# Attention, a 2-D FFT and a feed-forward: batch 1's first rows beside batch 0's spectral part, weights converted a whole piece at a time, tables loaded later

## The chip, the cores and the metric

One core of a Trainium2 chip. The time is device time in microseconds (us) of one launch. The engines of the core run side by side, each from its own queue in order: PE (TensorE: matmuls and transposes, into PSUM banks), DVE (VectorE), ACT (ScalarE), POOL (GpSimd), and SP, whose queue issues the DMAs. PEld is PE's loading of weights.

## The reference

```python
# q, k, v: (8, 12, 448, 64); w_ch1: (768, 3072); w_ch2: (3072, 768)
q_n, k_n = rmsnorm(q, g_q), rmsnorm(k, g_k)            # over the last axis
attn = softmax(q_n @ k_n.T / sqrt(64))                 # 448 x 448 per head
x = (attn @ v).transpose(0, 2, 1, 3).reshape(8, 448, 768)
mixed = real(fft(fft(x, axis=1), axis=2))
u = x + mixed
un = (u - mean(u)) / sqrt(var(u) + 1e-6)               # over the 768
out = u + maximum(un @ w_ch1, 0) @ w_ch2
```

All in float32; the weights arrive as 64-bit floats and are read as pairs of 32-bit words.

## The kernel before

The eight batches go through three parts each. `attention` works on pairs of heads (six pairs p): `transpose_pair` loads and normalises q and k (`norm_pair`: POOL raises the sums of squares to -1/2, tile ss; qkn is the product) and turns them into QT and KD; `softmax_pair` makes scores in four blocks of 112 rows (c), two heads each, tiles S: DVE takes the minimum of the negated scores (mn), ACT the exponential with its sum (P, sm), and P is scaled; `value_pair` transposes P (pt, copied to T) and multiplies by v (av) into xT. `fold` then adds and subtracts mirrored columns of xT (sd, eo, tot; DVE), and `spectral` does the two Fourier steps as matmuls with tables, D1 (tiles y, copied to Y) and D2 (tiles ab, joined to smdf), adds the residual (x, u) and normalises (un). `ffn` multiplies by the two weights: 24 pieces of w1 (tiles h, 18 matmuls each) and 36 of w2 (tiles o, 12 each). Where three matmuls stand for one, a float32 operand was split into a rounded part and a remainder.

A weight piece is converted once, during batch 0. `convert` loads the 64-bit words (dblw, line 650), then: ACT two operations (653, 654), DVE three (655, 659, 663, into magw), POOL an addition (667), ACT a rounding copy (668), POOL a subtraction (669), which gives the rounded part and the remainder (w). `converted` calls it for the two halves of a piece and stores the result in DRAM, from where later batches load it (line 713). The raw words lie in buffers "X", four of half a piece. 14 pieces (eight of w1, six of w2) are converted during batch 0's attention and spectral part (`convert_some`; their tiles have an e in the name), the other 46 during batch 0's feed-forward, up to three pieces of each weight ahead of use.

The order of work is that of Python generators: batch 0's `aux` (attention, then spectral) runs alone with the early conversions; then `merge` runs `ffn(b)` beside `aux(b + 1)`, a step of the one or the other by a ratio of costs. `aux(1)` begins there. A scheduler then places the instructions on each engine's queue by a timeline of its own, within the dependencies. PSUM banks are shared by tag: "S" (two banks) serves the scores, half of the y tiles, and all ab tiles.

`load_dft` is called at the second step of batch 0: it loads D1 and, as a staging tile d2s of 113 rows in one DMA, the second table; ACT rounds it into D2 and DVE forms the remainder.

Of the kernel before, what the change touches and what calls it, by code (L numbers as in the profile page):

```python
# [11 lines left out]
F32 = mybir.dt.float32  # L12
# [30 lines left out]
EARLY = 2  # L43
PLAIN_PAIRS = range(NPAIR)
# [43 lines left out]
def spectral_block(ctx, tc, q, k, v, g_q, g_k, w1, w2, d1, d2, out, nb=B):  # L88
# [63 lines left out]
    SLOTS = {"P": 8, "PT": 6, "X": 4, "M": 2, "unT": 6, "h": 6}  # L152

    def slot(tag, name, dtype=F32):
        return sb.tile([128, 900], dtype, tag=tag, name=name, bufs=SLOTS[tag])

# [12 lines left out]
    KL = cpool.tile([128, 2, S], F32R, name="KL")  # L169
# [8 lines left out]
    D2 = cpool.tile([N1, 2, 2, 2, N1], F32R, name="D2")  # L178
# [9 lines left out]
    def load_dft():  # L188
        nc.sync.dma_start(D1.rearrange("r i a n -> r (i a n)"), d1)
        st = slot("PT", "d2s")[:N1, : 4 * N1].rearrange("s (n t) -> s n t", n=4)  # L190
        nc.sync.dma_start(st, d2.rearrange("s (n t) -> s n t", n=4))
        d2v = D2.rearrange("s i c a t -> s (i c) a t")
        A.copy(d2v[:, :, 0], st)
        sub(d2v[:, :, 1], st, d2v[:, :, 0])
# [7 lines left out]
    FOLD_SLOTS = (("unT", "unT"), ("PT", "P"), ("M", "X"))  # L202
# [177 lines left out]
    def value_pair(b, p, Pc, xT):  # L380
# [6 lines left out]
        if plain(b, p):  # L387
# [3 lines left out]
            for h, a in enumerate((lo, hi)):  # L391
                av = bank("either" if b == 0 else "av", f"av{b}_{p}_{h}")
                for j in range(3):
                    pt = bank("PT", f"pt{b}_{p}_{h}_{j}")
                    for c in range(NC):
                        nc.tensor.transpose(
                            pt[:, c * C : (c + 1) * C],
                            Pc[c][:, 512 * h + j * 128 : 512 * h + (j + 1) * 128],
                            ident[:C, :C],
                        )  # L400
                    T = slot("PT", f"T{b}_{p}_{h}_{j}")[:, :S]
                    if (h * 3 + j) % 2 == 0:
                        V.tensor_copy(T, pt[:, :S])
                    else:
                        A.copy(T, pt[:, :S])
                    nc.tensor.matmul(
                        av[:D, :S], vhl[:, j, h], T, start=j == 0, stop=False
                    )
                    yield 1180
                nc.tensor.matmul(  # L410
                    av[:D, :S], vhl[a, 3, h], R[a], start=False, stop=True
                )
                A.copy(xT[a, p, :S], av[:D, :S])
                yield 760
# [35 lines left out]
    def attention(b, xT, EO):  # L450
# [3 lines left out]
        for p in range(NPAIR):  # L454
# [13 lines left out]
            if p > 3 and b != 1:  # L468
                fold(b, p - 4, xT, EO)
                yield 0  # L470
            values = value_pair(b, p, Pc, xT)
# [3 lines left out]
        for p in range(0 if b == 1 else 2, 3):  # L475
            fold(b, p, xT, EO)
# [3 lines left out]
    rstds = {}  # L480

    def fold(b, p, xT, EO):
# [5 lines left out]
        eo = slot(kept, f"eo{b}_{p}").rearrange("r (i t) -> r i t", i=2)  # L488
# [137 lines left out]
    uns = {}  # L626

    def aux(b):

        xT = sb.tile([128, NR, S + 2], F32, tag="xT", name=f"xT{b}", bufs=1)  # L630
        EO, uns[b] = [], {}
        yield from attention(b, xT, EO)
        yield from spectral(b, xT, EO, uns[b])
# [8 lines left out]
    def convert(src, bits, part, name):  # L642
# [4 lines left out]
        raw = slot("X", f"dbl{name}", U32)[:, : c * f].rearrange(  # L647
# [25 lines left out]
    class Stream:  # L673
# [18 lines left out]
        def converted(self, i, name):  # L692
# [5 lines left out]
            for c in (slice(0, self.n // 2), slice(self.n // 2, self.n)):  # L698
                convert(
                    src[:, c], bits[:, c], [hl[:, k, c] for k in range(2)],  # L700
                    f"{self.tag}{name}_{c.start}",
                )
# [252 lines left out]
```

## Time and profile before

| | us |
|---|---|
| median of 3 runs (lowest, highest) | 2242.81 (2241.82, 2243.02) |
| the profiled execution's own time | 2246.45 |
| its span, first to last instruction | 2244.7 |
| PE busy | 2107.8 (94%) |
| DVE busy | 1630.5 (73%) |
| ACT busy | 1074.2 (48%) |
| POOL busy | 576.2 (26%) |

How to read the rows shown later. A group row is: line, engine, operation, out<-in, partitions x elements, xcount | busy us, mean ns of one | idle time of the engine just before them, and what ended most of it. A wait row is: engine and the line that waited <- what released it: us in total, times, longest. A row in order of time is: start us, duration us, engine, line, operation, and in brackets the idle time before it with its releaser. A row of one tile's or line's instructions has the durations in ns as minimum/median/maximum, then the first and last start. Most DVE, ACT and POOL operations of the attention are recorded under line 111, a helper's line, so they are told apart by their tiles. In the profile buffer numbers are left out of tile names; D stands for both tables.

### The profile page before, as it was taken

The numbers are of one execution on the slowest core, as the hardware profiler recorded it, in microseconds if no ns is written. First come the engines' busy times: TensorE is split into PE (matmuls) and PEld (weight loads), VectorE is DVE, ScalarE is ACT, GpSimd is POOL, SyncE is SP. The second block draws the span as 40 slices with busy tenths as digits, with TensorE's granted clock in tenths as the row PEclk, the third lists the DMA queues.
The fourth block names the chain that finished last, engine by engine and source line by source line (L and its number), as shares of the span: only waits on it lengthen the run. The fifth ranks groups of instructions, "written<-read, shape, count | busy, mean of one in ns | idle before, by whom it ended". The sixth has DMA issues, their size and how long they took to land.

```text
span 2244.7 us, 32045 instructions
## 1 busy us (share of the span) xinstructions
PE 2107.8 (94%) x11164; PEld 1854.6 (83%) x11164; DVE 1630.5 (73%) x3281; ACT 1074.2 (48%) x2452; POOL 576.2 (26%) x442
## 2 busy tenths in 40 slices
PE   6887987769999999999999999999999999998997
PEld 3346866668999999999999999999999999998996
DVE  6896999888888577866788587867787588752122
ACT  5766776656554255524554355524554355421100
POOL 5883666854122021211121021101221022000000
PEclk7987988889999999999999999999999999999998
DMA  4556565557655575557655675558556674549664
GB/s 127 174 158 234 174 200 190 200 193 261 201 177 177 185 230 166 179 174 224 189 173 180 200 216 164 177 175 240 179 163 183 206 213 157 177 145 263 211 209 136
DMA packets 299188, 425.38 MB, mean 190 GB/s; under 512 B 187489, under 2 KB 225362, under 8 KB 299026
## 3 DMA queue, kind: packets, MB, share of 16 engines
q1 hardware_dynamic: 299026, 423.32, 61.0%
q8 instruction: 89, 1.46, 0.3%
q14 instruction: 73, 0.60, 0.1%
HBM read 363.47 MB, written 65.27 MB: 191 GB/s over the span
## 4 chain that ended last, share of the span: by engine, by line
PE 79%; DVE 9%; DMA 3%; ACT 2%; issue 2%; POOL 2%; SPq 0%; DVEq 0%; POOLq 0%; ACTq 0%
PE h L853 29%; PE o L874 28%; PE S L350 6%; PE av L439 4%; PE pt L427 4%; PE qk L313 1%; DMA w<-w 1%; PE y L530 1%; DVE mn L111 1%; DVE magw L663 1%; DMA dblw<-w 1%; PE oT L819 1%; DVE T L111 1%; DVE magw L655 1%; PE un L765 1%
## 5 line engine op out<-in xcount | busy, mean ns | idle before, releaser
L874 PE MATMUL o<-hs,w 128*128 128x448 f32 x3456 | 801.7, 374 | 24.5 <-DVE magw L655 6.8
L853 PE MATMUL h<-unT,w 128*128 128x448 f32 x3456 | 782.7, 371 | 6.0 <-POOL w L669 5.4
L874 PEld LDWEIGHTS o<-hs,w 128*128 128x128 f32 x3456 | 646.1, 191 | 84.0 <-ACT w L668 10.2
L853 PEld LDWEIGHTS h<-unT,w 128*128 128x128 f32 x3456 | 639.8, 189 | 59.7 <-POOL w L669 6.1
L111 ACT ACTIVATE P<-S,mn 112x448 f32<-112x448 f32 x384 | 243.1, 634 | 214.4 <-DVE mn L111 200.8
L111 POOL TENSOR_TENSOR qkn<-raw 112x1024 f32<-112x1024 f32 x47 | 89.8, 1912 | 731.1 <-PE qk L313 558.4
L111 DVE TENSOR_REDUCE mn<-S 112x1 f32<-112x448 f32 x384 | 233.3, 617 | 49.4 <-PE S L350 46.3
L111 ACT ACTIVATE hs<-h 128x448 fp32r<-128x448 f32 x192 | 104.4, 544 | 291.3 <-PE h L853 290.4
L111 DVE TENSOR_TENSOR acc<-o,acc 128x448 f32<-128x448 f32 x240 | 148.9, 621 | 109.5 <-PE o L874 107.8
L111 DVE SCALAR_TENSOR_TENSOR hs<-h,hs 128x448 fp32r<-128x448 f32 x192 | 119.3, 622 | 128.7 <-ACT hs L111 126.8
L439 PE MATMUL av<-T,vhl 128*128 128x448 f32 x504 | 179.9, 391 | 21.1 <-DVE T L111 11.6
L111 ACT CAST T<-pt 128x448 fp32r<-128x448 f32 x252 | 132.9, 533 | 135.3 <-PE pt L427 133.2
L111 POOL TENSOR_TENSOR ss<-ss,nhalf 112x16 f32<-112x16 f32 x48 | 150.0, 3125 | 112.9 <-DVE ss L111 109.6
L111 DVE TENSOR_TENSOR T<-pt,T 128x448 fp32r<-128x448 f32 x252 | 154.7, 617 | 27.8 <-ACT T L111 26.4
L111 DVE TENSOR_SCALAR P<-P,sm 112x448 f32<-112x448 f32 x336 | 158.0, 504 | 4.4
L427 PE MATMUL pt<-ident,P 112*128 112x112 f32 x1008 | 146.8, 262 | 1.5 <-DVE acc L111 1.5
L111 POOL TENSOR_TENSOR rstd<-st,nhalf 112x1 f32<-112x1 f32 (+2 forms) x32 | 18.5, 577 | 489.3 <-DVE st L111 489.3
L427 PEld LDWEIGHTS pt<-ident,P 112*128 112x128 f32 x1008 | 122.9, 143 | 23.0 <-DVE acc L111 2.1
L350 PE MATMUL S<-KD,QT 128*112 128x448 f32 x352 | 137.8, 393 | 2.0 <-ACT KD L111 1.6
L350 PE MATMUL S<-KL,QT 128*112 128x448 f32 x352 | 131.5, 376 | 2.6 <-DVE KL L111 2.5
L439 PEld LDWEIGHTS av<-T,vhl 128*128 128x128 f32 x504 | 95.7, 192 | 32.8 <-DVE T L111 14.9
L667 POOL TENSOR_TENSOR magw<-magw,dblw 128x256 uint32<-128x256 uint32 (+1 forms) x92 | 87.2, 956 | 73.6 <-DVE magw L663 50.4
(121 smaller groups left out, 2689.2 us busy)
## 6 DMA issues: line engine op xcount, KB each, us to landing
w<-w SPq DMA_DIRECT2D x288, 512.0 KB, 4.1
w<-w SPq DMA_DIRECT2D x192, 768.0 KB, 4.4
dblw<-w SPq DMA_DIRECT2D x60, 256.0 KB, 2.9
dblw<-w SPq DMA_DIRECT2D x32, 384.0 KB, 3.9
raw<-q SPq DMA_DIRECT2D x96, 112.0 KB, 4.3
raw<-k SPq DMA_DIRECT2D x96, 112.0 KB, 3.9
v<-v SPq DMA_DIRECT2D x96, 96.0 KB, 3.5
u_dram<-u SPq DMA_DIRECT2D x24, 336.0 KB, 3.5
```

The source lines that it names most:

```text
L111: ins = emit(*args, **kwargs)
L313: nc.tensor.transpose(pt[:, c * C : (c + 1) * C], qk[:, i, c].rearrange("t h d -> t (h d)"), ident[:C, :C],)
L350: ins = nc.tensor.matmul(s_, QT[:, h, cs], K[:, h], start=step == 0, stop=step == 1)
L427: nc.tensor.transpose(pt[:, c * C : (c + 1) * C], Pc[c][:, 512 * h + j * 128 : 512 * h + (j + 1) * 128], ident[:C, :C],)
L439: nc.tensor.matmul(av[:, :S], lv, T[:, i], start=(j == 0 and i == 0), stop=False)
L530: nc.tensor.matmul(o, src[:, par, t0 : t0 + n], D1[:, ri, par, cols], start=i != 1, stop=i != 0,)
L655: behind(nc.vector.tensor_scalar(out=value, in0=value, scalar1=MIN_HIGH, scalar2=MAX_HIGH, op0=ALU.max, op1=ALU.min,))
L663: behind(nc.vector.scalar_tensor_tensor(out=bits, in0=high, scalar=0xC0000000, in1=bits, op0=ALU.bitwise_and, op1=ALU.bitwise_or,))
L667: behind(nc.gpsimd.tensor_tensor(out=bits, in0=bits, in1=low, op=ALU.add))
L765: nc.tensor.transpose(pt[:, OFFS[i] : OFFS[i] + LENS[i]], uns[i][:, p * 128 : (p + 1) * 128], ident[: LENS[i], : LENS[i]],)
L853: pace(nc.tensor.matmul(o, w[:, a, c], unT[c][:, z], start=n == 0, stop=n == 17))
L874: pace(nc.tensor.matmul(o, w[:, a, f], hs[4 * g + f][:, z], start=n == 0, stop=n == 11))
```

## The change

Five edits.

- `aux(1)` is made at the start. Once batch 0's `spectral` begins, two of its steps are taken after each spectral step, up to 14; the rest runs beside `ffn(0)` as before. xT of a batch is now allocated after its first pair's scores.
- `convert` runs once per piece, with operations over the whole width (w1: 768 columns in place of 384 twice; w2: 512 in place of 256 twice). The buffers "X" are two of a whole piece in place of four of half a piece, of the same size in all; the folds of batches 2 and later, which lay in "X", take halves of such a buffer.
- `load_dft` is called at batch 0's step 40, and d2s is loaded by two DMAs, of 112 rows and of one.
- All copies of T in batch 0 are ACT's; before, every second one was DVE's.
- KL (remainder of K) and D2 are two parts of one tile, `rounded`; `load_gains` stands ahead of `load_pair(0, 0)`.

```diff
+DFT_STEP = 40
+AHEAD = 14
-    SLOTS = {"P": 8, "PT": 6, "X": 4, "M": 2, "unT": 6, "h": 6}
+    SLOTS = {"P": 8, "PT": 6, "M": 2, "unT": 6, "h": 6}
+    def wide(name, dtype=F32):
+        return sb.tile([128, 1800], dtype, tag="X", name=name, bufs=2)
...
-        nc.sync.dma_start(st, d2.rearrange("s (n t) -> s n t", n=4))
+        for r in rows_of(N1):
+            nc.sync.dma_start(st[r], d2[r].rearrange("s (n t) -> s n t", n=4))
...
-                    if (h * 3 + j) % 2 == 0:
-                        V.tensor_copy(T, pt[:, :S])
-                    else:
-                        A.copy(T, pt[:, :S])
+                    A.copy(T, pt[:, :S])
...
-        xT = sb.tile([128, NR, S + 2], F32, tag="xT", name=f"xT{b}", bufs=1)
         EO, uns[b] = [], {}
-        yield from attention(b, xT, EO)
-        yield from spectral(b, xT, EO, uns[b])
+        yield from attention(b, EO)
+        mixing.append(b)
+        yield from spectral(b, xTs[b], EO, uns[b])
...
-        raw = slot("X", f"dbl{name}", U32)[:, : c * f].rearrange(
+        raw = wide(f"dbl{name}", U32)[:, : c * f].rearrange(
...
-            for c in (slice(0, self.n // 2), slice(self.n // 2, self.n)):
-                convert(
-                    src[:, c], bits[:, c], [hl[:, k, c] for k in range(2)],
-                    f"{self.tag}{name}_{c.start}",
-                )
+            convert(src, bits, [hl[:, k] for k in range(2)], f"{self.tag}{name}")
...
+    load_gains()
     load_pair(0, 0)
-    load_gains()
     warm()
-    side = aux(0)
-    next(side)
-    load_dft()
-    for _ in side:
-        convert_some(CONVERT_EARLY)
+    second = aux(1)
+    ahead = iter(range(AHEAD if nb > 1 else 0))
+    for n, _ in enumerate(aux(0)):
+        if n == DFT_STEP:
+            load_dft()
+        if mixing:
+            for _ in range(2):
+                if next(ahead, None) is not None:
+                    next(second)
+        if n:
+            convert_some(CONVERT_EARLY)
...
-            aux(b + 1) if b + 1 < nb else iter(()),
+            second if b == 0 else aux(b + 1) if b + 1 < nb else iter(()),
```

How the built programs differ, at three places; line numbers are each kernel's own, and the number at a name's end is a buffer's.

DVE at the start of the program, before (raw, qkn, ss: batch 0, pair 0; D2 is the second table):

```order
L111 TENSOR_REDUCE ss0_0_139<-qkn0_0_137 112x16
L111 TENSOR_TENSOR raw0_0_110<-raw0_0_110,gneg_75 112x512
L111 TENSOR_SCALAR ss0_0_139<-ss0_0_139 112x16
L111 TENSOR_TENSOR D2_78<-d2s_159,D2_78 113x4x113
L111 TENSOR_TENSOR qkn0_0_137<-raw0_0_110,ss0_0_139 112x2x4x64 x2
L111 TENSOR_TENSOR QT0_0_163<-qk0_0_0_165,QT0_0_163 64x448 x2
```

The same place on DVE now:

```order
L113 TENSOR_REDUCE ss0_0_137<-qkn0_0_135 112x16
L113 TENSOR_TENSOR raw0_0_112<-raw0_0_112,gneg_75 112x512
L113 TENSOR_SCALAR ss0_0_137<-ss0_0_137 112x16
L113 TENSOR_TENSOR qkn0_0_135<-raw0_0_112,ss0_0_137 112x2x4x64 x2
L113 TENSOR_TENSOR QT0_0_156<-qk0_0_0_158,QT0_0_156 64x448 x2
```

The table's subtraction, and ACT's copy ahead of it, have gone from the head of their queues to pair 2 of batch 0's attention.

PE in batch 0's spectral part, from the end of the y tiles to the ab tiles, before:

```order
L530 MATMUL y0_1_1_1521<-D1_77,eo0_0_1140 112x2x65
L530 MATMUL y0_1_1_1521<-D1_77,eo0_1_1362 112x2x65
L530 MATMUL y0_1_1_1521<-D1_77,tot0_1369 112x65
L603 MATMUL ab0_0_0_1531<-Y0_0_0_1498,D2_78 113x390 x3
L603 MATMUL ab0_0_1_1535<-Y0_1_1_1528,D2_78 113x390 x3
L603 MATMUL ab0_1_0_1589<-Y0_0_1_1508,D2_78 112x390 x3
L603 MATMUL ab0_1_1_1593<-Y0_1_0_1518,D2_78 112x390 x3
```

PE from the last of the y tiles to the ab tiles now (S1_0 are scores of batch 1, pair 0; rows 0 and 1 stand above this piece, among the y tiles):

```order
L546 MATMUL y0_1_0_1415<-D1_77,tot0_1259 113x65
L357 MATMUL S1_0_2_0_1462<-KD1_0_1196,QT1_0_1195 112x448
L357 MATMUL S1_0_2_0_1462<-rounded_66,QT1_0_1195 112x448
L357 MATMUL S1_0_2_1_1463<-KD1_0_1196,QT1_0_1195 112x448
L357 MATMUL S1_0_2_1_1463<-rounded_66,QT1_0_1195 112x448
L619 MATMUL ab0_0_0_1476<-Y0_0_0_1368,rounded_66 113x390 x3
L619 MATMUL ab0_0_1_1480<-Y0_1_1_1432,rounded_66 113x390 x3
L357 MATMUL S1_0_3_0_1527<-KD1_0_1196,QT1_0_1195 112x448
L357 MATMUL S1_0_3_0_1527<-rounded_66,QT1_0_1195 112x448
L357 MATMUL S1_0_3_1_1528<-KD1_0_1196,QT1_0_1195 112x448
L357 MATMUL S1_0_3_1_1528<-rounded_66,QT1_0_1195 112x448
L320 MATMUL qk1_1_0_1515<-ident_68,qkn1_1_1435 128x112 x4
```

Score rows 2 and 3 of batch 1 now stand ahead of the ab tiles of token halves 0 and 1; before, the first score row of batch 1 stood behind the first h.

POOL in batch 0's feed-forward, at the conversion of pieces 10 and 11 of w1, before:

```order
L667 TENSOR_TENSOR magw1_10_2503<-magw1_10_2503,dblw1_10_0_2504 128x384
L667 TENSOR_TENSOR magw1_10_2503<-magw1_10_2503,dblw1_10_3_2514 128x384
L111 TENSOR_TENSOR qkn1_4_3030<-raw1_4_2537 112x1024
L669 TENSOR_TENSOR w1_10_2502<-magw1_10_2503,w1_10_2502 128x384 x2
L667 TENSOR_TENSOR magw1_11_2592<-magw1_11_2592,dblw1_11_0_2593 128x384
L111 TENSOR_TENSOR raw1_4_2537<-raw1_4_2537,gneg_75 112x512
L667 TENSOR_TENSOR magw1_11_2592<-magw1_11_2592,dblw1_11_3_2603 128x384
L669 TENSOR_TENSOR w1_11_2591<-magw1_11_2592,w1_11_2591 128x384
```

The same place on POOL now:

```order
L684 TENSOR_TENSOR magw1_10_2396<-magw1_10_2396,dblw1_10_2397 128x768
L113 TENSOR_TENSOR qkn1_4_2661<-raw1_4_2267 112x1024
L686 TENSOR_TENSOR w1_10_2395<-magw1_10_2396,w1_10_2395 128x768
L684 TENSOR_TENSOR magw1_11_2451<-magw1_11_2451,dblw1_11_2452 128x768
L113 TENSOR_TENSOR raw1_4_2267<-raw1_4_2267,gneg_75 112x512
```

Two operations of half the width became one of the whole width, at much the same place among the attention's operations.

More of the change, by code (lines that the diff above doesn't have):

```diff
@@ L165, in rows_of @@
         return [slice(a, z) for a, z in ((0, n - n % 16), (n - n % 16, n)) if a < z]
-    KL = cpool.tile([128, 2, S], F32R, name="KL")
+    rounded = cpool.tile([128, 2 * S + 8 * N1], F32R, name="rounded")
+    KL = rounded[:, : 2 * S].rearrange("r (h t) -> r h t", h=2)
     G.memset(KL.bitcast(F32), 0.0)
@@ L177, in spectral_block @@
     D1 = cpool.tile([128, 2, 2, 5 * NI], F32, name="D1")
-    D2 = cpool.tile([N1, 2, 2, 2, N1], F32R, name="D2")
+    D2 = rounded[:N1, 2 * S :].rearrange("s (i c a t) -> s i c a t", i=2, c=2, a=2)
     u_dram = dram.tile([2, 4, N1, DM], F32, name="u_dram")
@@ L199, in spectral_block @@
     X_BANKS = (("either", "either"), ("either", "either"))
-    FOLD_SLOTS = (("unT", "unT"), ("PT", "P"), ("M", "X"))
+    FOLD_SLOTS = (("unT", "unT"), ("PT", "P"), ("M", None))
     loaded = {}
@@ L448, in value_pair, with attention @@
         A.copy(xT[:, p, S : S + 1], xT[:, p, 0:1])
-    def attention(b, xT, EO):
+    xTs = {}
+    def attention(b, EO):
         yield from transpose_pair(b, 0)
@@ L468, in attention @@
             if p > 3 and b != 1:
-                fold(b, p - 4, xT, EO)
+                fold(b, p - 4, xTs[b], EO)
                 yield 0
-            values = value_pair(b, p, Pc, xT)
+            if p == 0:
+                xTs[b] = sb.tile([128, NR, S + 2], F32, tag="xT", name=f"xT{b}", bufs=1)
+            values = value_pair(b, p, Pc, xTs[b])
             for x in ahead:
@@ L475, in attention @@
         for p in range(0 if b == 1 else 2, 3):
-            fold(b, p, xT, EO)
+            fold(b, p, xTs[b], EO)
             yield 0
     rstds = {}
+    halves = {}
     def fold(b, p, xT, EO):
@@ L487, in fold @@
         once = slot(short, f"sd{b}_{p}").rearrange("r (i e t) -> r i e t", i=2, e=2)
-        eo = slot(kept, f"eo{b}_{p}").rearrange("r (i t) -> r i t", i=2)
+        if kept is not None:
+            eo = slot(kept, f"eo{b}_{p}")
+        else:
+            if p % 2 == 0:
+                halves[b] = wide(f"eo{b}_{p}")
+            eo = halves[b][:, p % 2 * 900 : p % 2 * 900 + 900]
+        eo = eo.rearrange("r (i t) -> r i t", i=2)
         add(eo[:, 0, :449], xT[:, p, :449], xT[:, p + 3, :449])
@@ L626, in spectral_block @@
     uns = {}
+    mixing = []
     def aux(b):
-        xT = sb.tile([128, NR, S + 2], F32, tag="xT", name=f"xT{b}", bufs=1)
         EO, uns[b] = [], {}
-        yield from attention(b, xT, EO)
-        yield from spectral(b, xT, EO, uns[b])
+        yield from attention(b, EO)
+        mixing.append(b)
+        yield from spectral(b, xTs[b], EO, uns[b])
     NF = DFF // 128
```

## The prediction

> **What bounds the kernel now.** I read the table of stretches first, because the share of the whole span (PE 94%) is a mean over stages with different limits. Columns: length, then busy time (and instructions) of PE, PEld, DVE, ACT and POOL, granted clock, DMA share, GB/s.
>
> ```profile
> core 0: us, PE busy (x) PEld busy (x) DVE busy (x) ACT busy (x) POOL busy (x), PEclk, DMA share, GB/s
> 20.00:160.00 140.00, 116.64 (x425) 51.62 (x426) 127.54 (x264) 106.66 (x265) 109.87 (x77) 0.83 0.53 156
> 160.00:196.00 36.00, 19.42 (x91) 16.70 (x91) 24.59 (x51) 15.38 (x31) 17.97 (x18) 0.59 0.57 188
> 196.00:546.00 350.00, 283.46 (x1388) 245.56 (x1387) 310.44 (x623) 239.08 (x570) 220.68 (x213) 0.89 0.62 207
> 1000.00:1500.00 500.00, 499.94 (x2799) 458.06 (x2798) 377.54 (x763) 233.29 (x522) 78.47 (x44) 1.00 0.62 189
> ```
>
> Four stages. Batch 0's attention (20 to 160) is tight on every engine. Batch 0's spectral part (160 to 196) is a chain: no engine is busy for 70% of it. Batch 0's feed-forward, with batch 1 beside it and 46 of the 60 weight pieces still to convert (196 to 546), is held by DVE: 310.4 of 350 us, PE idle for 66.5. From there on PE is full, as the last row shows. So whatever is won or lost before 546 us reaches the end one to one, and nothing is to be won after it.
>
> Next the waits. They say in whose name PE and POOL idle in the long stage (engine and line, releaser: us in total, times, longest), and who holds the loads of raw weights on SP's queue. The last two rows are PE's own, in order of time: batch 1's first y, and the first matmul of the feed-forward.
>
> ```profile
> POOL magw L667 <- DVE magw L663: 50.4, 36, 6.4
> ACT dblw L654 <- DMA dblw<-w: 18.8, 17, 2.9
> SPq L650 <- POOL magw L667: 116.9, 74, 7.0
> 491.57 3.81 PE L530 MATMUL y<-D,eo 128*113 128x130 f32 x16 [14.66 <-DVE eo L111]
> 196.68 0.74 PE L853 MATMUL h<-unT,w 128*128 128x448 f32 x1
> ```
>
> DVE is late for POOL's part of the conversion and for batch 1's folds (eo), on which PE stands for 14.7 us.
>
> **The start.** The tables' load (d2s) stands at the head of ACT's queue, and DVE's subtraction behind it.
>
> ```profile
> 18.63 0.57 ACT L111 CAST D<-d2s 113x452 fp32r<-113x452 f32 x1 [16.61 <-DMA d2s<-d]
> 10.82 2.93 POOL L111 TENSOR_TENSOR ss<-ss,nhalf 112x16 f32<-112x16 f32 x1 [8.72 <-DVE ss L111]
> 19.23 0.63 DVE L111 TENSOR_TENSOR D<-d2s,D 113x452 fp32r<-113x452 f32 x1 [8.56 <-ACT D L111]
> 19.78 1.29 DVE L111 TENSOR_TENSOR qkn<-raw,ss 112x512 f32<-112x512 f32 x2
> ```
>
> The first normalisation multiply needs only POOL's power, done at 10.82 + 2.93 = 13.75, yet it starts at 19.78. With the tables later it starts 6.0 us earlier, and PE's first transposes with it. The tables' two operations (0.57 on ACT, 0.63 on DVE) now fall into pair 2 of the busy attention stage, and the third pair's loads stand behind the loads of v on SP, as they did. Bounds: -6.0, or 0 if those loads gate the stage. I take -5. Moving the gains ahead in the code leaves SP's order as it was and costs nothing.
>
> **Whole pieces.** Clean durations of a half piece in two widths, 256 columns (w2) and 384 (w1); the middle figure is the median in ns:
>
> ```profile
> L655 DVE TENSOR_SCALAR magw1e<-magw1e x16: 331/351/1084, 33.4 to 186.5; 128x384 f32<-128x384 f32 x16
> L655 DVE TENSOR_SCALAR magw2e<-magw2e x12: 273/281/289, 85.7 to 133.8; 128x256 f32<-128x256 f32 x12
> L659 DVE TENSOR_SCALAR magw1e<-magw1e x16: 345/348/3080, 35.7 to 187.6; 128x384 uint32<-128x384 uint32 x16
> L659 DVE TENSOR_SCALAR magw2e<-magw2e x12: 279/283/735, 87.2 to 136.5; 128x256 uint32<-128x256 uint32 x12
> L663 DVE SCALAR_TENSOR_TENSOR magw1e<-dblw1e,magw1e x16: 531/546/1284, 36.3 to 188.0; 128x384 uint32<-128x384 uint32 x16
> L663 DVE SCALAR_TENSOR_TENSOR magw2e<-dblw2e,magw2e x12: 410/415/1189, 88.2 to 138.0; 128x256 uint32<-128x256 uint32 x12
> L667 POOL TENSOR_TENSOR magw1e<-magw1e,dblw1e x16: 1002/1025/1858, 37.0 to 188.7; 128x384 uint32<-128x384 uint32 x16
> L667 POOL TENSOR_TENSOR magw2e<-magw2e,dblw2e x12: 733/742/1585, 89.2 to 138.9; 128x256 uint32<-128x256 uint32 x12
> 33.38 0.62 DVE L655 TENSOR_SCALAR magw1e<-magw1e 128x384 f32<-128x384 f32 x2
> ```
>
> 128 columns more cost 0.070, 0.065 and 0.131 us on DVE, so at zero width 0.141, 0.153 and 0.153 remain: 0.447 us a piece that the second half pays today. That is the upper end. Two in a row take 0.62, not 2 x 0.35, so 0.08 of each is overlapped already: 0.447 - 0.24 = 0.21 is the lower end. I take 0.3, between the two, as the halves stand partly in a row and partly apart: 46 x 0.3 = 14 us of DVE in the long stage, 14 x 0.3 = 4 in the attention. POOL's first operation saves 0.742 - 2 x 0.283 = 0.18 a piece; POOL (220.7 of 350) isn't the bound.
>
> [...]
>
> Against this stands a wait between DVE and POOL. First L655 in the long stage (598 ns where 351 is clean), then the softmax multiply there and in the PE-bound stage (700 to 1900):
>
> ```profile
> L655 DVE TENSOR_SCALAR magw<-magw 128x384 f32<-128x384 f32 x32 | 18.6, 598 | 0.2
> L111 DVE TENSOR_SCALAR P<-P,sm 112x448 f32<-112x448 f32 x26 | 19.4, 751 | 0.4
> L111 DVE TENSOR_SCALAR P<-P,sm 112x448 f32<-112x448 f32 x228 | 96.8, 464 | 3.1
> 186.47 1.08 DVE L655 TENSOR_SCALAR magw1e<-magw1e 128x384 f32<-128x384 f32 x1 [0.28 <-ACT magw1e L653]
> 186.32 1.02 POOL L667 TENSOR_TENSOR magw1e<-magw1e,dblw1e 128x384 uint32<-128x384 uint32 x1 [1.08 <-DVE magw1e L663]
> ```
>
> The last two rows show it: DVE's 0.35 us operation took 1.08 and ended at 187.55, just after POOL's at 187.34. A POOL operation of a whole piece lasts nearly twice as long, so each such wait doubles. For the conversions half as many instructions wait, which cancels. The softmax multiplies stay as many: 26 x (0.751 - 0.464) = 7.5 us is their wait today, and 7.5 more is what the change adds. [...]
>
> **Four rows of batch 1 ahead.** 14 steps move from the long stage into the spectral one: all score rows of pair 0 and half of pair 1's transposes.
>
> ```profile
> L111 DVE TENSOR_REDUCE mn<-S 112x1 f32<-112x448 f32 x52 | 31.6, 614 | 10.6 <-PE S L350 10.4
> L111 ACT ACTIVATE P<-S,mn 112x448 f32<-112x448 f32 x48 | 30.2, 631 | 10.4 <-DVE mn L111 10.3
> L111 DVE TENSOR_REDUCE ss<-qkn 112x16 f32<-112x1024 f32 x29 | 35.2, 1214 | 0.7
> ACT w1e L668 <- POOL magw1e L667: 14.2, 5, 9.3
> PE ab L603 <- ACT Y L111: 6.8, 2, 3.4
> ```
>
> On DVE: 8 minima x 0.614 = 4.9, 4 multiplies x 0.464 = 1.9, one sum 1.2, two subtractions of QT about as long as a minimum, 1.2, and eight tiny operations, an estimate of 1.3: 10.5 us leave the long stage. Where they go, DVE is free for 36 - 24.6 = 11.4 us, so they fit, but not for nothing. The scores share the two S banks with y and ab: y0_1_0 now stands behind rows 0 and 1, ab0_0 behind row 2, ab0_1 behind row 3. A row holds a bank for its minimum and its exponential, 0.614 + 0.631 and two matmuls, about 2 us; with both heads through one DVE and one ACT about 2.8. Four rows are at most 11 us. At the low end they cost 0: the chain already waits 6.8 us for ACT's copies of Y, which stand behind casts that wait 14.2 us for POOL, and two of those casts are now one. I take +5, the middle, as both waits are of the same size.
>
> **The copies of T.** All 36 of batch 0 are now ACT's:
>
> ```profile
> L111 DVE COPY T<-pt 128x448 f32<-128x448 f32 x18 | 11.1, 616 | 6.2 <-PE pt L396 6.2
> L111 ACT COPY T<-pt 128x448 f32<-128x448 f32 x18 | 9.5, 527 | 1.4 <-PE pt L396 1.3
> ```
>
> DVE in the attention stage goes from 127.5 by 11.1 and 4 to 112, ACT from 106.7 to about 111 (9.5 more, less for the merged operations). If DVE alone set the pace the stage would shrink by 15/127.5 of 140 = 16 us; if the copies now queue behind ACT's casts, it grows by some 4. PE (116.6) and POOL (109.9) stand just below, so I take -5.
>
> **The sum.** Long stage: DVE 310.4 - 14 - 10.5 + 7.5 = 293.4 us; at today's share (310.4/350 = 0.887) that is 331, so -19, taken as -20. With 20.6 in place of 14 and no longer waits it is 279.3, so 315: -35. Start -5, attention -5, spectral +5, long stage -20: -25 us. The profiled execution took 2246.45 us (span 2244.7), so 2221; it lies 3.6 above the median of 2242.81, and for the median I predict 2218. A change under 0.2% (4.5 us) can't be told from none here.
>
> **Rivals.**
> - Slower: two whole buffers in place of four halves for the raw weights. SP waited in 74 cases for a buffer, so they were always full: 350 x 4/92 = 15.2 us is a half's stay. The loads by size (KB each, median us to land):
>
> ```profile
> dblw<-w SPq DMA_DIRECT2D x60, 256.0 KB, 2.9
> dblw<-w SPq DMA_DIRECT2D x32, 384.0 KB, 3.9
> w<-w SPq DMA_DIRECT2D x288, 512.0 KB, 4.1
> w<-w SPq DMA_DIRECT2D x192, 768.0 KB, 4.4
> ```
>
>   A half lands in 3.2 and has some 2.9 of work (DVE 0.98 or 1.25, POOL 0.74 or 1.03, ACT two operations of about half a us), which leaves 9 us of standing in queues. A whole piece needs 4.3 to land, like the loads of its size, and 4.6 of work; at 7.5 us in queues it stays 16.4, and 46/2 of those are 377 us: +27, in all +22, 2264. It decides where the gains elsewhere are gone: stage at 355, stay 15.4, standing 6.5 us. Against it: half of today's standing is behind the sister half, and DVE's load falls. 12 in 100.
> - Larger gain: DVE's and PE's waits shrink together. PE's floor in the stage is 283.5 less 6 of moved scores; at 90% busy that is 308, -42; with -6, -9 and +2 elsewhere, 2188. For it: PE's 14.7 us wait for folds sits in this stage. 15 in 100.
> - A wash: rows ahead cost the full 11 us, the conversions' saving goes into the waits with POOL, and the stage wins 12, the start 5: 2237. 21 in 100, of which 8 lie within 0.2%.
> - That the steps don't move is excluded: the built order has them between y and ab.
>
> **How the numbers follow.** My forecast holds 52 in 100 and its own range is 2200 to 2231 (long stage -35 to -12, attention -10 to 0). Faster: 52 + 15 + 13 = 80; same 8; slower 12. The range of 2190 to 2245 leaves out most of the slow rival and the edge of the large one.
>
> **What would show it.** Right: the first qk transposes near 14.5 us; batch 0's first h 3 to 7 us earlier than 196.7; y1 about 25 us earlier than 491.6; DVE below 300 us in that stage, with the whole-piece L655 of 768 columns near 0.56 when undisturbed and the softmax multiply above 0.75. Wrong: ACT's or POOL's waits for dblw far over 18.8 us (the buffers bind), the first h later than 197 (the banks bind), or PE's idle time before its full stage at 66 us as before.

## The result and the profile after

The changed kernel takes 2229.0 us against 2242.7: a ratio of 0.9944, 95% interval 0.9929 to 0.9959, so 0.0056 x 2243 = 12.6 us less. The prediction said 2218, within 2190 to 2245: the direction came out, the size is about half. The profiled execution's span fell from 2244.7 to 2227.2 us; 3.6 us of these 17.5 are before's own excess over its median (2246.45 against 2242.81).

First the table of stretches of the kernel after, cut at its own milestones: the attention of batch 0 up to its first x, the spectral part up to the first h, the long stage up to the first h of batch 1, and a piece of the stage in which PE is full (columns as in the prediction). Behind it stand the same first three stretches of the kernel before, with the borders that this cut gives there.

```profile
20.00:148.10 128.10, 102.19 (x404) 44.17 (x402) 117.00 (x195) 106.48 (x241) 92.92 (x51) 0.93 0.54 164
148.10:194.60 46.50, 23.81 (x121) 20.25 (x121) 38.00 (x72) 24.37 (x48) 20.07 (x13) 0.70 0.42 132
194.60:537.40 342.80, 281.36 (x1382) 244.53 (x1383) 293.91 (x481) 217.84 (x422) 192.92 (x122) 0.89 0.64 215
1000.00:1500.00 500.00, 499.52 (x2793) 458.14 (x2793) 377.62 (x765) 233.55 (x524) 78.40 (x44) 1.00 0.62 189
```

```profile
20.00:154.70 134.70, 114.43 (x417) 49.73 (x417) 122.30 (x255) 106.66 (x265) 104.65 (x76) 0.84 0.53 158
154.70:196.70 42.00, 22.27 (x101) 18.88 (x101) 30.20 (x61) 15.99 (x33) 23.32 (x20) 0.58 0.56 182
196.70:546.30 349.60, 283.13 (x1387) 245.57 (x1388) 310.07 (x622) 238.78 (x571) 220.55 (x213) 0.89 0.62 207
```

In the long stage DVE's load fell by 16.2 us to 293.9, which the prediction had to half a us (293.4; in part by luck, as shown below). But the stage fell by 6.8 us only, from 349.6 to 342.8: DVE's share went from 0.887 down to 0.857. PE idles for 61.4 us in it, 66.5 before. The spectral part got 4.5 us longer, the attention ends 6.5 us earlier.

The rows of time behind these borders, from the kernel after: the first multiply of the normalisation and the first transposes, the first x and the first h of batch 0, batch 1's first y, the end of the long stage. Then from the kernel before its first x and its end of the long stage.

```profile
13.77 1.29 DVE L113 TENSOR_TENSOR qkn<-raw,ss 112x512 f32<-112x512 f32 x2 [3.12 <-POOL ss L113]
14.52 0.60 PE L320 MATMUL qk<-ident,qkn 112*128 112x112 f32 x4 [3.16 <-DVE qkn L113]
148.15 0.91 PE L578 MATMUL x<-ident,xr 128*113 128x128 f32 x6 [1.77 <-ACT xr L113]
194.56 0.74 PE L866 MATMUL h<-unT,w 128*128 128x448 f32 x1 [0.38 <-DVE magw L672]
470.31 0.67 PE L546 MATMUL y<-D,eo 128*113 128x130 f32 x4 [1.04 <-DVE eo L113]
537.43 1.38 PE L866 MATMUL h<-unT,w 128*128 128x448 f32 x6
```

```profile
154.66 1.20 PE L562 MATMUL x<-ident,xr 128*113 128x128 f32 x4 [1.79 <-ACT xr L111]
546.31 0.86 PE L853 MATMUL h<-unT,w 128*128 128x448 f32 x3
```

Batch 1's first y comes 21.3 us earlier (491.57 before), and the wait of 14.7 us for its folds is down to 1.04. Yet the stage's end comes only 8.9 us earlier: from y to the end it takes 67.1 us, 54.7 before. More than half of what was won on batch 1's side is given back behind it.

The view of waits, for the long stage alone (us in total, times, longest), of the kernel after:

```profile
POOL magw L684 <- DVE magw L680: 47.9, 23, 9.3
POOL w L686 <- ACT w L685: 45.6, 30, 6.8
ACT magw L670 <- DMA dblw<-w: 26.6, 16, 3.8
ACT dblw L671 <- DMA dblw<-w: 11.5, 10, 2.6
ACT w L685 <- POOL magw L684: 25.9, 14, 4.0
```

And of the kernel before, as far as the prediction didn't show them:

```profile
POOL w L669 <- ACT w L668: 18.9, 20, 2.4
ACT magw L653 <- DMA dblw<-w: 2.7, 2, 1.7
ACT w L668 <- POOL magw L667: 19.8, 17, 5.4
```

ACT's wait for raw weights rose from 18.8 (in the prediction) and 2.7, 21.5 in all, to 38.1; POOL's wait for ACT's cast from 18.9 to 45.6. A load lands as fast as expected (median 4.3 and 4.4 us). The prediction had named ACT's wait far over 18.8 us as the sign that the buffers bind.

SP's own queue holds the loads of raw weights and the stores of finished pieces (w) in one order. Its two longest waits in the long stage after, and the second of them before (the first, 116.9, is in the prediction):

```profile
SPq L667 <- POOL magw L684: 101.2, 36, 7.4
SPq L716 <- POOL w L686: 89.4, 40, 5.1
```

```profile
SPq L703 <- POOL w L669: 56.6, 35, 5.7
```

The loads wait 15.7 us less for their buffers, and the stores 32.8 us more for POOL's result. So a load may also be late because it stands behind a store on SP. No kernel moves the stores to another queue, so this cause is not told apart from the buffers.

### The profile page after: what moved, and what is told of

It is laid out like the page before. It is cut to its first block, busy times and chain, and to the rows that moved or that the text cites. A ratio compares the mean times of both kernels' runs of the same rounds, so it can differ in the third digit from the quotient of the medians.

```text
span 2227.2 us, 31403 instructions
## 1 busy us (share of the span) xinstructions
PE 2092.4 (94%) x11164; PEld 1847.3 (83%) x11164; DVE 1612.1 (72%) x3083; ACT 1060.8 (48%) x2290; POOL 536.6 (24%) x322
## 4 chain that ended last, share of the span: by engine, by line
PE 77%; DVE 10%; DMA 4%; ACT 4%; issue 2%; POOL 2%; SPq 0%; DVEq 0%; POOLq 0%; ACTq 0%
PE h L866 29%; PE o L887 27%; PE S L357 6%; PE av L443 4%; PE pt L431 4%; DMA dblw<-w 2%; PE y L546 1%; PE qk L320 1%; POOL magw L684 1%; DVE mn L113 1%; ACT P L113 1%; DMA w<-w 1%; DVE sm L113 1%; DVE eo L113 1%; PE oT L832 1%
## 5 line engine op out<-in xcount | busy, mean ns | idle before, releaser
L866 PEld LDWEIGHTS h<-unT,w 128*128 128x128 f32 x3456 | 646.7, 190 | 61.3 <-ACT w L685 7.1
L887 PEld LDWEIGHTS o<-hs,w 128*128 128x128 f32 x3456 | 639.4, 189 | 68.1 <-issue 6.0
L113 DVE TENSOR_SCALAR P<-P,sm 112x448 f32<-112x448 f32 x336 | 164.9, 525 | 4.7
L357 PE MATMUL S<-rounded,QT 128*112 128x448 f32 x352 | 132.2, 377 | 1.7 <-DVE rounded L113 1.6
L443 PEld LDWEIGHTS av<-T,vhl 128*128 128x128 f32 x504 | 95.5, 190 | 24.7 <-DVE T L113 11.4
L113 DVE TENSOR_SCALAR sm<-sm 112x2 f32<-112x2 f32 x192 | 60.3, 314 | 59.0 <-ACT P L113 56.6
```

The costliest lines, as they stand in the source:

```text
L113: ins = emit(*args, **kwargs)
L357: ins = nc.tensor.matmul(s_, QT[:, h, cs], K[:, h], start=step == 0, stop=step == 1)
L443: nc.tensor.matmul(av[:, :S], lv, T[:, i], start=(j == 0 and i == 0), stop=False)
L866: pace(nc.tensor.matmul(o, w[:, a, c], unT[c][:, z], start=n == 0, stop=n == 17))
L887: pace(nc.tensor.matmul(o, w[:, a, f], hs[4 * g + f][:, z], start=n == 0, stop=n == 11))
```

## The experiments

Theories: A, pieces are slow because a whole piece is passed from engine to engine; B, the fixed cost of operations is on the path, and what it saves was given back to the two whole buffers; C, long POOL operations hold up DVE; D, the two whole buffers bind; E, the rows ahead only moved; F, a slot of T is worth as much as a faster release. All differences from the kernel before are ratios times 2243 us; borders of the stages are the first x, the first h, and the first h of batch 1, as above.

| kernel | ratio to before (95%) | first qk | first x | first h | long stage | DVE busy in it |
|---|---|---|---|---|---|---|
| before | 1 | 20.5 | 154.7 | 196.7 | 349.6 | 310.1 |
| after | 0.9944 (0.9929 to 0.9959) | 14.5 | 148.1 | 194.6 | 342.8 | 293.9 |
| half operations | 1.0022 (1.0008 to 1.0035) | 14.2 | 154.1 | 198.5 | 359.1 | 305.1 |
| POOL in halves | 0.9965 (0.9951 to 0.9979) | 15.3 | 145.4 | 191.3 | 350.1 | 290.8 |
| three buffers, six slots of P | 1.0598 (1.0576 to 1.0621) | 14.4 | 180.7 | 237.8 | 350.7 | 299.5 |
| two buffers, six slots of P | 1.0634 (1.0610 to 1.0659) | 14.5 | 179.7 | 236.3 | 358.9 | 307.1 |
| before with whole pieces alone | 0.9994 (0.9982 to 1.0007) | 19.6 | 157.8 | 194.3 | 351.6 | 302.9 |
| no rows ahead | 0.9995 (0.9982 to 1.0007) | 14.8 | 150.7 | 191.8 | 356.8 | 295.0 |
| early release, five slots of T | 0.9932 (0.9910 to 0.9955) | 14.1 | 149.7 | 195.5 | 341.3 | 303.1 |
| five slots of T | 1.0016 (1.0003 to 1.0029) | 14.6 | 151.5 | 197.2 | 362.7 | 306.7 |
| early release, six slots of T | 1.0040 (1.0025 to 1.0054) | 14.9 | 168.9 | 208.1 | 358.5 | 307.9 |
| the same, POOL in halves early | 1.0011 (1.0000 to 1.0023) | 14.1 | 154.2 | 194.7 | 360.1 | 305.0 |
| before with T on ACT alone | 1.0021 (1.0008 to 1.0034) | 20.8 | 157.8 | 195.2 | 355.1 | 305.3 |
| tables early | 0.9967 (0.9953 to 0.9980) | 14.3 | 146.2 | 193.2 | 348.0 | 301.3 |

**Half operations in whole buffers.** The load stays whole, the operations are issued per half again:

```
+            raw = load_raw(src, ...)
+            for c in (slice(0, self.n // 2), slice(self.n // 2, self.n)):
+                convert(raw[:, c], bits[:, c], [hl[:, k, c] for k in range(2)])
-            convert(src, bits, [hl[:, k] for k in range(2)], ...)
```

> The changed kernel with one thing undone: each piece is still loaded whole into one of two whole buffers, but its eight operations are again issued per half. Theory A (hand to hand: a whole piece is passed from ACT to DVE to POOL to ACT to POOL, so with whole operations each engine waits for a longer one before it): DVE's load in the long stage rises by about 14 us to 308, but POOL's wait for ACT's cast falls from 45.6 us to about 20 and the stage ends at 343 to 347 us as in the changed kernel (342.8); whole time 2226 to 2233, against 2229. Theory B (the fixed cost of DVE's operations is on the path, and the missing gain was lost to the two buffers): 14 us more on DVE at a share of 0.857 make the stage 16 us longer; whole time about 2245. ACT's wait for the loads stays near 38 us in both.

Its long stage in the table of stretches, and from its waits there that of POOL for the cast and those of ACT for the loads:

```profile
198.50:557.60 359.10, 282.28 (x1395) 245.17 (x1396) 305.09 (x636) 236.11 (x570) 230.34 (x216) 0.89 0.62 204
```

```profile
POOL w L690 <- ACT w L689: 39.0, 34, 6.2
ACT magw L674 <- DMA dblw<-w: 18.2, 14, 3.6
ACT dblw L675 <- DMA dblw<-w: 9.4, 11, 3.4
```

The stage is 16.3 us longer, to the point what B said, and the whole time 0.0078 of 2243, 17.5 us. A falls: POOL's wait for the cast fell to 39.0 only, not to 20, and the time rose. Whole operations do save about what the prediction priced; DVE's load is 11.2 us lower with them (305.1 to 293.9; priced at 14). ACT's wait for the loads was expected near 38 us and is 27.6, in a stage that is longer: this wait alone does not tell how long the stage is. Set beside before, the kernel suggests that the load in one costs something: the same halves, four rows of batch 1 gone ahead, and still 9.5 us more than before's 349.6. Tables, copies of T and rows ahead differ too, so that is not a measure of it.

**Whole pieces alone, and no rows ahead.** The first is the kernel before with one load and one operation for each piece; the second the changed kernel with one number changed:

```
-            for c in (slice(0, self.n // 2), slice(self.n // 2, self.n)):
-                convert(src[:, c], bits[:, c], [hl[:, k, c] for k in range(2)], ...)
+            convert(src, bits, [hl[:, k] for k in range(2)], ...)
```

```
-AHEAD = 14
+AHEAD = 0
```

> The kernel before with the whole pieces alone: one load into one of two whole buffers and one operation each, and nothing else of the change. Theory D (two whole buffers cost about what the whole operations save): half operations in two whole buffers made the long stage 359.1 us with the rows ahead, whole operations 342.8; without the rows ahead 12 us (10.5 us of DVE at a share of 0.887) come on top, so 355 against 349.6 before, and the whole time is 2244 to 2250 against 2242.7. Theory B, the sum of the forecast (14 us of DVE saved, 7.5 lost in longer waits, 4 won in the attention): stage 342, whole time about 2232.

> The changed kernel with no rows of batch 1 ahead of its feed-forward stage; all else as changed. The forecast's terms: the spectral part of batch 0 is 4.4 us shorter (first x to first h 42 us in place of 46.5), the long stage has 10.5 us more of DVE, at a share of 0.857 12 us longer (355), whole time 2237 against 2229. Rival E (the rows only moved, as what sets the long stage is the stream of pieces through the buffers and not DVE's load): long stage 343 to 347, whole time 2225 to 2229.

The long stage of the first:

```profile
194.30:545.90 351.60, 285.84 (x1385) 245.85 (x1385) 302.89 (x491) 222.75 (x434) 196.56 (x122) 0.88 0.62 209
```

That of the second, and its first h in order of time:

```profile
191.80:548.60 356.80, 291.49 (x1388) 250.63 (x1389) 295.01 (x488) 222.62 (x431) 196.22 (x120) 0.87 0.61 204
```

```profile
191.85 0.71 PE L866 MATMUL h<-unT,w 128*128 128x448 f32 x1 [3.51 <-DVE unT L113]
```

Whole pieces alone bring nothing (0.9994, the interval holds 1). DVE's load fell by 7.2 us as the forecast's terms say (-14 + 7.5 = -6.5), and the stage became 2.0 us longer all the same. So the load was right and its worth was not. B's 2232 for this kernel, the sum of the forecast's terms, is outside what was measured. D's 2244 to 2250 is nearer and still misses it: 0.9994 of 2243 is 2241.7 (2239.0 to 2244.6), and the stage is 351.6 and not D's 355.

The rows ahead are worth 0.0051 of 2243, 11.4 us: without them the change is worth nothing (0.9995). In the stages they cost 5.4 in the spectral part (41.1 us without, 46.5 with) and win 14.0 in the long one. E falls. But the 14.0 does not come from DVE's load, which is 295.0 without the rows and 293.9 with them, where 10.5 less was forecast. PE is busy for 291.5 and 281.4 us, with 1388 and 1382 matmuls, and idle for 65.3 and 61.4: 10.1 of the 14.0 is PE's busy time, at a granted clock of 0.87 and 0.89. What links the rows ahead to it was not found.

**Three buffers against two.** The third whole buffer needs room, which two slots of P give in both:

```
-        return sb.tile([128, 1800], dtype, tag="X", name=name, bufs=2)
+        return sb.tile([128, 1800], dtype, tag="X", name=name, bufs=3)
-    SLOTS = {"P": 8, ...
+    SLOTS = {"P": 6, ...
```

> The changed kernel with three whole buffers for the raw weights in place of two; to make room, the tag of the softmax rows has six slots in place of eight. To be read against the next kernel, which has the six slots and two buffers. Theory D (two buffers bind): ACT's wait for the loads in the long stage falls from about 38 us to below 15, the stage shortens by 6 to 12 us against its control, and the whole time with it. Theory A (pieces are late because of the engines that pass them on): the loads come earlier but the stage is within 2 us of its control.

> The control of the kernel with three buffers: the changed kernel with six slots for the softmax rows in place of eight and two whole buffers. Theories A and D say the same of it: rows wait for slots in batch 0's attention, so it is 0 to 15 us slower than the changed kernel (2229 to 2244), and ACT's wait for the loads in the long stage is near 38 us as there.

ACT's waits for raw weights in the long stage, with three buffers:

```profile
ACT dblw L671 <- DMA dblw<-w: 14.0, 15, 2.9
```

And with two:

```profile
ACT magw L670 <- DMA dblw<-w: 16.2, 14, 2.8
ACT dblw L671 <- DMA dblw<-w: 13.2, 10, 3.8
```

29.4 us of waiting became 14.0, and the stage is 8.2 us shorter (358.9 to 350.7): within D's 6 to 12, though not far above the scatter that the last pair of kernels shows. The whole time differs by 0.0036, 8 us. Both lie 134 us or more above before, where 0 to 15 us over the changed kernel was expected of the control. Six slots of P cost the later batches too: behind the first h of batch 1 PE idles for 78.2 us in the control and for 17.7 in the changed kernel.

**Early release.** The scaled low words go to a tile of their own, and the buffer of raw weights is free after DVE's third operation:

```
+        tail = sb.tile([128, 768], U32, tag="tail", ..., bufs=1)
-        behind(nc.scalar.activation(low, low, AF.Copy, scale=2.0**-29))
+        behind(nc.scalar.activation(tail, low, AF.Copy, scale=2.0**-29))
...
-        behind(nc.gpsimd.tensor_tensor(out=bits, in0=bits, in1=low, op=ALU.add))
+        behind(nc.gpsimd.tensor_tensor(out=bits, in0=bits, in1=tail, op=ALU.add))
-    SLOTS = {..., "PT": 6, ...
+    SLOTS = {..., "PT": 5, ...
```

> The changed kernel with the scaled low words written to a tile of their own in place of the buffer of raw weights, so that a buffer comes free after DVE's third operation and no longer after POOL's addition; to make room, the tag of T has five slots in place of six. To be read against the next kernel, which has the five slots alone. Theory D (a whole buffer is held too long): a buffer is held for at least 1.4 to 2.1 us less (POOL's addition), the wait of the loads for POOL's addition is gone, and the long stage is 5 to 12 us shorter than in the control. Rival: the pieces are held up by the engines that pass them on, and the stage is within 2 us of the control's, as the tile of low words (one) now waits for POOL in place of the buffer.

> The control of the kernel with the early release: the changed kernel with five slots in place of six for the tag of T. All theories say the same: the attention waits for slots a little more, 0 to 20 us slower than the changed kernel (2229 to 2249).

The long stage with the release, and ACT's wait for raw weights there:

```profile
195.50:536.80 341.30, 284.19 (x1378) 248.19 (x1379) 303.07 (x477) 217.71 (x419) 200.14 (x122) 0.88 0.65 213
```

```profile
ACT magw L670 <- DMA dblw<-w: 17.2, 12, 3.7
```

The same two views of the control:

```profile
197.20:559.90 362.70, 288.74 (x1388) 248.75 (x1388) 306.69 (x490) 222.63 (x428) 195.87 (x125) 0.88 0.61 204
```

```profile
ACT magw L670 <- DMA dblw<-w: 20.6, 15, 3.2
ACT dblw L671 <- DMA dblw<-w: 12.4, 8, 2.8
```

The release takes 21.4 us off the stage (0.0084 x 2243 = 18.8 off the whole), above D's 5 to 12, with ACT's wait for the loads halved (33.0 to 17.2) as with the third buffer. D is borne out in direction twice. How the release helps is open: on SP the loads wait for DVE's third operation (124.0 us) as long as the control's wait for POOL's addition (123.4), and it is the wait of the stores for POOL's result that falls, from 74.9 to 54.7. The size of D is not settled either: the control's long stage is itself 19.9 us longer than that of the changed kernel with its six slots, the release brings the kernel back to where the changed one stands (0.9932 against 0.9944, the intervals overlap), and why one slot of T costs so much was not found. No kernel here is measurably faster than the changed one.

The same release with the slots kept, the low words in T's own tag (`tail = slot("PT", ...)`), and then POOL's two operations in halves while batch 0's attention runs:

> The changed kernel with the early release, the tile of low words now taken from the tag of T, which keeps its six slots. Theory D: the long stage was 362.7 us with five slots and 341.3 with the early release beside them; against the changed kernel's 342.8 the same cure gives 325 to 335, whole time 2211 to 2221 against 2229. Rival F (a slot of T is worth about what the release is worth: five slots alone cost 20 us): the low words take a slot away from T for as long as a piece is under way, and the whole time is 2225 to 2235.

> The kernel before this one in the list (early release, six slots) with POOL's two operations per half for the pieces converted before the feed-forward stages alone. Theory C, in the attention: POOL's halves brought the first h from 194.6 to 191.3 us, so the first h comes 3 us earlier than in that kernel, the long stage is as long as there, and the whole time is 3 us lower. Rival (the 3 us are the scatter of the attention's order between kernels): within 2 us of it, either way.

Both ranges are missed. 1.0040 of 2243 is 2252: the release wins nothing here, which goes F's way, but the loss is larger than F's 2225 to 2235. The first x comes at 168.9, 20.8 us later than in the changed kernel, and PE's longer wait for T in the attention is 7.6 us of that. The row of its waits, and then that of the changed kernel:

```profile
PE av L410 <- ACT T L113: 19.5, 11, 7.8
```

```profile
PE av L410 <- ACT T L113: 11.9, 10, 2.5
```

POOL's halves brought the first h 13.4 us earlier there and 6.5 us in the whole (0.0029), more than C's 3. All of the 13.4 lies in the attention, where the granted clock was 0.89 against 0.81 in the one execution of each that was profiled, so how much of it is POOL's halves was not settled.

**POOL in halves throughout.** The changed kernel, with each of POOL's two operations issued as two:

```
+        for z in (slice(0, c // 2), slice(c // 2, c)):
+            behind(nc.gpsimd.tensor_tensor(out=bits[:, z], in0=bits[:, z], in1=low[:, z], op=ALU.add))
-        behind(nc.gpsimd.tensor_tensor(out=bits, in0=bits, in1=low, op=ALU.add))
```

> The changed kernel with POOL's two operations of a piece issued per half, all others whole. Theory C (DVE is held up for as long as a POOL operation lasts, so long POOL operations cost DVE): the softmax multiply in the long stage falls from a mean of 858 ns to about 750 (24 x 0.108 = 2.6 us), DVE's whole-piece operations fall too, the folds of batch 0 are no longer at 2 to 4 us, and the whole time is 5 to 8 us lower, 2221 to 2224, although POOL pays some 0.18 us more for each operation (46 x 2 x 0.18 = 17 us of POOL in the stage). Theory A (the order in which a piece is passed on decides, not the hold): POOL's busy time rises by those 17 us and the time is 2229 to 2234.

Its first h in order of time, and its long stage:

```profile
191.25 0.74 PE L871 MATMUL h<-unT,w 128*128 128x448 f32 x1
```

```profile
191.30:541.40 350.10, 285.53 (x1397) 248.36 (x1397) 290.80 (x498) 224.23 (x432) 225.45 (x216) 0.89 0.64 212
```

C holds up to the first h (3.3 us earlier) and in DVE's load (290.8, 3.1 us less; the softmax multiply's mean is 733 ns where 750 was expected). The time does not follow: the stage is 7.3 us longer, the whole 0.0021, 4.7 us, though the intervals of the two kernels overlap. 0.9965 of 2243 is 2235, far from C's 2221 to 2224 and just above A's 2229 to 2234. This is the kernel with DVE's smallest load of all, and its long stage is not short; POOL's busy time rose from 192.9 to 225.5 in it. That POOL's longer work is the reason wasn't tested.

**T on ACT alone, and the tables early.** The first is the kernel before with every plain copy of T on ACT; the second the changed kernel with the tables loaded ahead of the attention, still in two loads of 112 and 1 rows:

```
-                    if (h * 3 + j) % 2 == 0:
-                        V.tensor_copy(T, pt[:, :S])
-                    else:
-                        A.copy(T, pt[:, :S])
+                    A.copy(T, pt[:, :S])
```

```
-DFT_STEP = 40
+DFT_STEP = 0
```

> The kernel before with all copies of T on ACT, and nothing else of the change. The forecast put the copies and the whole pieces together at -5 us in the attention. The kernel with the whole pieces alone had its first x 3.1 us later than before (its start 0.9 us earlier), so whole pieces cost about 4 there, and the changed kernel's attention won 0.5 in all: the copies should be worth about -4.5, first x near 150 against 154.7, long stage as before within 2 us, whole time 2236 to 2241 against 2243. Rival (the copies queue behind ACT's casts for the conversions): first x 154 to 158, whole time 2242 to 2247.

> The changed kernel with the tables loaded at the start, as before; all else as changed. The forecast's start term (-5, bounds -6 to 0): the first transposes of q and k go back from 14.5 to about 20.5 us, and if the start gates what follows, first x and first h come 5 to 6 us later and the whole time is 2234 to 2235 against 2229. Rival (the start is made up by the attention, which waits for its loads or its slots anyway): first x within 2 us of the changed kernel's 148.1, whole time 2227 to 2231. A third reading, scatter: with the copies of T alone undone or done, the long stage moved by 5 us though no instruction of it was changed, so it may move by as much here, 338 to 348 against 342.8, in either direction.

The long stage with T on ACT alone:

```profile
195.20:550.30 355.10, 286.63 (x1376) 245.78 (x1376) 305.29 (x617) 235.54 (x562) 221.81 (x212) 0.88 0.63 206
```

That of the tables early, and from its start the cast of the tables and the first transposes:

```profile
193.20:541.20 348.00, 284.14 (x1385) 244.21 (x1386) 301.30 (x481) 219.68 (x422) 201.17 (x124) 0.88 0.63 212
```

```profile
11.56 0.57 ACT L113 CAST rounded<-d2s 113x452 fp32r<-113x452 f32 x1 [0.61 <-DMA d2s<-d]
14.31 1.20 PE L320 MATMUL qk<-ident,qkn 112*128 112x112 f32 x8 [3.17 <-DVE qkn L113]
```

T alone gains nothing: first x at 157.8, whole time 4.7 us longer. The copies are no cure by themselves.

The tables early are the surprise: the first transposes stay at 14.3. With its load split, the cast starts at 11.56, where the single load of 113 rows let it start at 18.63 (in the prediction). The three kernels that load it early and unsplit (before, whole pieces alone, T on ACT alone) have their first transposes at 19.6 to 20.8. So the split alone wins the start, and the later place adds nothing to it; about 20.5 had been expected. The whole time of 2236 comes near the 2234 to 2235 of the first reading, but not for its reason, as the start was not lost.

All the same the kernel is 5 us slower than the changed one in whole (0.9967 against 0.9944, intervals that overlap), and its long stage 5.2 us longer with nearly the same instructions in it. T alone shows the same: 5.5 us in a stage that holds the same 36 split copies of T, and nothing of the edit. The edits move the order of work even so: in the traces of tables early and of the changed kernel, DVE's operations stand in a different order at places up to about 600 us. Which of the moves costs the 5 us was not found. From these two pairs I take about 5 us of the long stage as scatter from one built order to the next.

## Why the prediction came out as it did

- **The start (-5).** -6.0 (20.52 to 14.52). The size was right, the reason half wrong: the load was late because it went as one load of 113 rows. In one piece (before) it was issued at 5.84 and took 12.77 us to land, so the cast started at 18.63; in 112 and 1 rows (tables early), issued from 5.84 too, the cast started at 11.56. Why the one piece took longer was not shown: how many DMA engines a load used is in no row here.
- **The attention (-5).** -0.5, since the first x comes 6.5 earlier and the start is 6.0 of it. The bounds were -16 to +4. Whole pieces alone made it 4 us longer (first x 3.1 later with a start 0.9 earlier) and T alone 2.8; together, in the changed kernel, nearly nothing. The parts don't add. What failed is the load itself: 15 us were to leave DVE, and from the first instruction to the first x it is busy for 125.7 us where it was 126.8. The copies of T and part of the conversions did leave; the softmax multiplies, 24 in both, grew by 5.4 us, a term that the prediction counted in the long stage and put at nothing here. Before and after:

```profile
L111 DVE TENSOR_SCALAR P<-P,sm 112x448 f32<-112x448 f32 x24 | 17.6, 731 | 0.2
```

```profile
L113 DVE TENSOR_SCALAR P<-P,sm 112x448 f32<-112x448 f32 x24 | 23.0, 959 | 0.4
```

- **The spectral part (+5).** +4.5; the rows alone 5.4. Right.
- **The long stage (-20).** -6.8: the term that was mis-sized. DVE's load came out (293.9 for 293.4), and that is partly luck, as two errors cancel. Added up by groups, DVE's operations of the conversion fell from 128.8 to 101.9 us. In such a sum, time in which two operations overlap counts twice, and that double count is 7.6 smaller after; so I estimate that the conversion saved about 19, where 14 was forecast. The rest of DVE's work should have fallen by 3.0 (-10.5 + 7.5) and rose by 3.1. Eight minima went ahead, but three more of batch 2 came in at the stage's end; and the softmax multiply's mean rose from 751 to 858 ns, 24 x 0.107 = 2.6 us where 7.5 was expected. Other operations that the change leaves as they were grew as well, one of them nearly threefold, here behind the softmax multiply after, and then alone before:

```profile
L113 DVE TENSOR_SCALAR P<-P,sm 112x448 f32<-112x448 f32 x24 | 20.4, 858 | 0.5
L113 DVE TENSOR_SCALAR ss<-ss 112x16 f32<-112x16 f32 x6 | 6.1, 1022 | 0.1
```

```profile
L111 DVE TENSOR_SCALAR ss<-ss 112x16 f32<-112x16 f32 x6 | 2.2, 368 | 0.1
```

  What failed is the step "at today's share": load divided by 0.887. Over the kernels above the share lies between 0.83 (POOL in halves, no rows ahead) and 0.89, and the load does not order them: 290.8 us gave 350.1, 303.1 gave 341.3. Split up, the rows ahead won 14.0 (forecast 10.5/0.887 = 12; the number agrees by luck, since DVE's load differs by 1.1 and not by 10.5), and the whole pieces with the rest lost 7.2 (356.8 without the rows against 349.6) where -7.3 was forecast ((-14 + 7.5)/0.887); of the 7.2, whole pieces alone are 2.0 and the remaining 5.2 no more than the scatter. What takes the place of the divided load is shown in part: the way of a piece through the buffers costs time, by two pairs of kernels, but its size is not settled.

  The price of an operation was right as well. DVE's three operations of a whole w1 piece in the changed kernel, where nothing disturbs them (the middle figure is the median in ns):

```profile
L672 DVE TENSOR_SCALAR magw1e<-magw1e x8: 530/550/2183, 26.9 to 183.9; 128x768 f32<-128x768 f32 x8
L676 DVE TENSOR_SCALAR magw1e<-magw1e x8: 543/546/560, 29.1 to 184.5; 128x768 uint32<-128x768 uint32 x8
L680 DVE SCALAR_TENSOR_TENSOR magw1e<-dblw1e,magw1e x8: 945/952/1909, 29.7 to 185.5; 128x768 uint32<-128x768 uint32 x8
```

  Against two halves each (351, 348 and 546 in the prediction) that is 0.152, 0.150 and 0.140 less, 0.442 a piece, the upper end that was given (0.447); 11.2/46 = 0.243 is what the half operations showed of it in the whole load, near the lower end (0.21), where 0.3 was taken. That 0.243 is a balance too: it holds what other operations lost.
- **The rival of the two buffers.** It was given 12 in 100 as the end of the gain. Its mechanism shows in direction, its price didn't reach its point: a third buffer took 8.2 us off the stage and an early release 21.4 off its control. The prediction argued against it that half of the standing is behind the sister half. Whole operations win 16.3, and whole pieces alone end 2.0 behind before; if they win as much there, a buffer that comes free only as one costs some 18. That is an estimate: no kernel had the load in one as its only edit.
- **The whole.** 2229.0 lies in the forecast's own range of 2200 to 2231, though its long stage does not (-6.8, where -35 to -12 was given). Of the signs that it named, the first transposes, DVE below 300 us and the longer softmax multiply came; the first h came 2.1 us earlier and not 3 to 7, batch 1's first y 21.3 and not 25; and ACT's wait for the loads, the sign of the rival, came as well.
- **Nothing after 546.** The next batch's stage is 246.3 us in place of 249.0, but holds 17 matmuls fewer (1376 for 1393), which PE did earlier: the border moved, not the speed. The rows of that stage, after and then before:

```profile
537.40:783.70 246.30, 246.30 (x1376) 226.04 (x1375) 181.35 (x369) 113.18 (x252) 39.09 (x22) 1.00 0.62 190
```

```profile
546.30:795.30 249.00, 249.00 (x1393) 227.98 (x1391) 188.78 (x383) 116.59 (x262) 39.14 (x22) 1.00 0.62 189
```

  In the two profiled executions the same border of batch 6 (its first h, at 1779.9 and 1792.5 us) stands 12.6 us apart, and the ends 17.5. So 4.9 us arise behind 1790 us. Late weight loads do not explain them: PE waits 4.9 us for one there before, and 4.0 us for two after.

## What to carry to other kernels

A load on the busiest engine turns into time only if that engine sets the end (here 16.2 us less work on DVE made the long stage 6.8 us shorter, and 7.2 less, with whole pieces alone, made it 2.0 longer); where four engines pass pieces round through two buffers, price the buffer's stay as its own term, and don't divide a load by today's share. Pull work of the next stage into a chain that leaves engines idle: 14 steps here paid 5.4 us and won 14.0. When a forecast load comes out, check its parts: here two errors cancelled. Before believing 5 us of one edit, build a second kernel whose edit shouldn't touch the stage, and see how much it moves.

## What the runs showed of the hardware

The granted clock of the attention stage was 0.84 before, 0.93 after, and 0.81 in the early release with six slots, whose row is:

```profile
20.00:168.90 148.90, 115.34 (x405) 47.22 (x404) 121.98 (x198) 107.36 (x243) 99.93 (x56) 0.81 0.52 157
```

PE's busy time for nearly the same matmuls moved with it (114.4 us for 417, 102.2 for 404, 115.3 for 405), as did the stage's length (134.7, 128.1, 148.9). So part of what looks like a gain or loss of an edit in this stage goes with the clock that PE was granted in that one execution; whether a stage with more waits is granted less, or waits more because of it, these runs don't tell apart. The long stage shows the same in small: PE was busy there for 281.4 us after, at 0.89, and for 291.5 without the rows ahead, at 0.87, with 6 matmuls more.

The load of 113 rows in one piece (199.5 KB, before) was issued at 5.84 us, took 12.77 us and held its user back until 18.63; the same bytes in two loads, 112 rows and one (197.8 and 1.8 KB, tables early), issued from 5.84, released it by 11.56.
